# A third raw weight buffer, the first expert's weights split later and in thirds, and a planner's extra delay kept for its lowest rank alone

## Chip, cores, metric

One core of one Trainium2 chip runs the whole program. The metric is device time in microseconds (us): the median of three runs, 2241.27 us before (2236.84 to 2241.68). TensorE is called PE (PEld for its weight loads), VectorE DVE, ScalarE ACT, GpSimd POOL, and SyncE, which issues the DMAs, SP.

## What is computed

A gated linear attention feeds a mixture of experts, which feeds a last block with a cosine:

```python
for t in range(S):                                   # attention, B=4 H=8 S=768 D=48
    state = alpha[:, :, t, :, None] * state + k_t (x) v_t
    y[:, :, t] = q_t @ state
x = y as [3072, 384]
P = exp(x @ w_gate - max)                            # then 8 rounds of row and column scaling
out = sum over 8 experts e of P[:, e:e+1] * (relu(x @ w1[e]) @ w2[e])       # 1024 hidden
h = out @ w_in                                       # 2048 hidden
return (h * cos(h)) @ w_out
```

## The kernel before

**Tiles.** Tokens run along the free dimension. The attention goes by units of 256 tokens (12 units) and, in each, by 4 pairs of heads: 48 slots. `ew` prepares a slot two slots ahead: on DVE two scans along segments of 32 tokens, scalings and a reciprocal, on POOL three 128x256 products or differences, on ACT copies. The slot itself makes on PE 4 transposes (112 columns), 8 score products (48x48), 8 key-value products (64x64) and, one slot later, 8 output products (48x64); DVE puts a mask on the scores (two copy_predicated) and steps the state (four 128x48 scalar_tensor_tensor), ACT copies.

**Passes.** The experts are passes 0 to 7, the two halves of the last block passes 8 and 9. A pass holds its weights in 4 chunks (c) of two matrices (i = 0 first layer, 1 second), each split in a high part (fp32r) and a low part: names w<c><i>h and w<c><i>l, 128x768 each. A product is three: high by high, high by low, low by high. `Passes.first` makes 9 matmuls for one of 8 hidden tiles (ft), then the activation (`act_relu`: ACT writes the high part, DVE the low part; `cos` in passes 8 and 9: four ACT, four DVE and one POOL instruction), and `Passes.second`, two hidden tiles later (three in the last passes), 9 matmuls of the second layer (12 with 384 columns in passes 8 and 9). Pass 0 has 256-token blocks that run between the slots of the attention, as soon as a unit's four slots are done; passes 1 to 9 have 6 blocks of 512 tokens. Pass 0 has 1,728 such matmuls of 256 columns, and 72 more make the gate's logits; `sinkhorn` and `spread` then make the gates P.

**Weights.** `Weights.load` brings a 128x768 piece into one of two raw buffers, `Weights.prep` splits it (ACT copies the high part, POOL subtracts it for the low part) and issues the load for the buffer that it has freed. In the last block of a pass, two preps follow each odd ft. For pass 0 all eight preps stand ahead of the attention's loop.

**Order.** Everything is recorded into `Plan`, which replays it in a simulation of its own with a cost for each instruction (`_cost`) and a latency between engines (`LAT`), and so fixes each engine's order: of the instructions that are ready, the lowest rank first, then the oldest. Attention's slots, activations, evictions and splits of x are rank 0, the passes' matmuls and weight preps rank 1, `ew` and the first preps rank 2, decoding, the adding up of alpha and its loads rank 3. `rank(r, True)` also makes an instruction wait for the last recorded matmul (a floor). What a consumer gets as extra delay in that simulation stands in `Plan.issue`:

```python
same = self.ops[u][0] == e
late = 0 if same or not self.ops[u][6] or self.ops[u][0] == "tensor" else 4000 if e == "sync" else 2500
ready[u] = max(ready[u], t + cost + ((0 if e == "tensor" else 60) if same else self.LAT[e]) + late)
```

`ops[u][6]` is the consumer's rank: every consumer of rank 1 or more, but matmuls, is taken to be ready 2500 ns later (4000 ns behind a DMA) than the latency says. On the chip each engine then works off its list in order. All instructions are issued on line 180, so groups of the profile are told by tiles.

Of the kernel before, what the change touches and what calls it, by code (L numbers as in the profile page):

```python
# [9 lines left out]
F32 = mybir.dt.float32  # L10
# [5 lines left out]
ALU = mybir.AluOpType  # L16
# [3 lines left out]
B, H, S, D = 4, 8, 768, 48  # L20
# [3 lines left out]
E = 8  # L24
NPAIR = H // 2
CH = 64
NPASS = E + 2
NCH = 4
FT = 8
NT = NTOK // 128  # L30
UN = 256
UNITS = [(b, s, UN) for b in range(B) for s in range(0, S, UN)]
BLK = 512
CW = 768
AMIN, AMAX = 0.25, 1.0
LAG = 2
LAG3 = 3
NRAW = 2
FARENA, RARENA = 10000, 10240
SEG = 32  # L40
SCAN = (SEG + 1) * (UN // SEG)
DBG = None
# [20 lines left out]
class Plan:  # L63
# [81 lines left out]
    def issue(self):  # L145
        n = len(self.ops)
        left = [len(o[5]) for o in self.ops]
        users = [[] for _ in range(n)]
        for i, o in enumerate(self.ops):
            for j in o[5]:  # L150
                users[j].append(i)
        ready = [0.0] * n
        cand = {e: [] for e in self.LAT}
        free = dict.fromkeys(self.LAT, 0.0)
        for i, o in enumerate(self.ops):
            if not left[i]:
                cand[o[0]].append(i)
        self.times = [0.0] * n
        for _ in range(n):
            best = None  # L160
            for e, c in cand.items():
                if not c:
                    continue
                t = max(free[e], min(ready[i] for i in c))
                if best is None or t < best[0]:
                    best = t, e
            t, e = best
            i = min((i for i in cand[e] if ready[i] <= t), key=lambda i: (self.ops[i][6], i))
            cand[e].remove(i)
            eng, name, args, kw, cost, _, _ = self.ops[i]  # L170
            self.times[i] = t
            free[e] = t + cost
            for u in users[i]:
                same = self.ops[u][0] == e
                late = 0 if same or not self.ops[u][6] or self.ops[u][0] == "tensor" else 4000 if e == "sync" else 2500
                ready[u] = max(ready[u], t + cost + ((0 if e == "tensor" else 60) if same else self.LAT[e]) + late)
                left[u] -= 1
                if not left[u]:
                    cand[self.ops[u][0]].append(u)
            getattr(getattr(self.nc, eng), name)(*args, **kw)  # L180
# [10 lines left out]
class Arena:  # L191
# [17 lines left out]
    def ring(self, n, shape, dtype):  # L209
        return ring([self.tile(shape, dtype) for i in range(n)])  # L210
# [8 lines left out]
class Weights:  # L219
# [15 lines left out]
    def prep(self):  # L235

        if self.prepped == len(self.order):
            return
        e = self.k.e
        p, c, i = key = self.order[self.prepped]  # L240
        self.prepped += 1
        r = self.raw.pop(key)
        hi, lo = self.t[key] = self.k.w[c][i]
        e.scalar.copy(hi, r)
        e.gpsimd.tensor_tensor(out=lo, in0=r, in1=hi.bitcast(F32), op=ALU.subtract)
        self.load()


# [63 lines left out]
class Kernel:  # L312
    def __init__(self, tc, ctx, qka, vv, nat, vt, wts, w8, wg, cst, out):
        self.tc, self.nc, self.ctx = tc, tc.nc, ctx
        self.qka, self.vv, self.nat, self.vt, self.wts, self.w8 = qka, vv, nat, vt, wts, w8
        self.wg, self.cst, self.out = wg, cst, out

        def pool(name, bufs):
            return ctx.enter_context(tc.tile_pool(name=name, bufs=bufs))

        const = pool("const", 1)
        self.e = self.nc
        self.w = [[[const.tile([128, CW], F32R, name=f"w{c}{i}{z}") for z in "hl"] for i in range(2)] for c in range(NCH)]
        self.raw = [const.tile([128, CW], F32, name=f"raw{i}") for i in range(NRAW)]
        self.ident = const.tile([128, 128], F32, name="ident")
        self.ones = const.tile([128, 128], F32, name="ones")
        self.Lg = const.tile([128, NT, E], F32, name="Lg")
        self.P = const.tile([128, NT, E], F32, name="P")
        self.pt = ctx.enter_context(tc.tile_pool(name="pt", bufs=1, space=bass.MemoryType.DRAM)).tile([NT * E, 128], F32, name="pt")
        self.w32 = ctx.enter_context(tc.tile_pool(name="w32", bufs=1, space=bass.MemoryType.DRAM)).tile([2, NCH, 2, 128, CW], F32, name="w32")  # L330
        self.fbuf = const.tile([128, FARENA], F32, name="fbuf")
        self.rbuf = const.tile([128, RARENA], F32R, name="rbuf")
        self.mask = const.tile([128, UN], U8, name="mask")
        psum = ctx.enter_context(tc.tile_pool(name="psum", bufs=1, space=PSUM))
        self.bank = [psum.tile([128, 512], F32, name=f"bank{i}") for i in range(8)]
        self.flag = const.tile([1, 1], I32, name="flag")
        self.x = const.tile([128, KT, NTOK], F32, name="x")
        self.acc = const.tile([128, KT, NTOK], F32, name="acc")
# [48 lines left out]
    def attention(self, pool):  # L387
        e = self.e
        V, A, G, T, SP = e.vector, e.scalar, e.gpsimd, e.tensor, e.sync
        nt0 = UN // CH  # L390
# [2 lines left out]
        xt = pool.ring(4, [128, 2, UN], F32)  # L393

        decs, fwds, bwd, self.heads = pool.ring(2, [128, SCAN + 1], F32), pool.ring(2, [128, SCAN], F32), pool.tile([128, SCAN + 1], F32), pool.tile([128, SCAN], F32)
        rps, tots = pool.ring(2, [128, UN // SEG], F32), pool.ring(3, [128, nt0], F32)
        kts = pool.ring(2, [128, nt0, D], F32)
        yts = pool.ring(1, [128, UN], F32)
        adev = pool.tile([128, NPAIR * len(UNITS)], F32)
        m1, m2 = tots()[:, 0:1], tots()[0:1, 0:1]  # L400

        late = [Arena(self.acc[:, k, NTOK - 4 * UN:]) for k in range(KT)]

        k6s, mask = late[0].ring(3, [128, UN + CH], F32), self.mask
        qka = ring([z.tile([128, 3, UN], F32) for z in late[1:] + [pool, pool]])
        pt0 = self.bank[0][:, :nt0 * 112].rearrange("p (t d) -> p t d", d=112)
        pk = self.bank[2][:, :nt0 * D].rearrange("p (t d) -> p t d", d=D)
        pg0, py0 = (self.bank[i][:, :UN] for i in (1, 3))
# [73 lines left out]
        for i in range(len(slots) + 1):  # L482
# [3 lines left out]
            if i < len(slots):  # L486
# [6 lines left out]
                t, k6, X, tot = st["qk"], st["k6"], st["X"], st["tot"]  # L493
# [94 lines left out]

    def sinkhorn(self, sm, ps):
        V, A, T = self.e.vector, self.e.scalar, self.e.tensor  # L590
        P, Lg, ones = self.P, self.Lg, self.ones
        self.rank(0)
        mx, nm, m1 = (sm.tile([128, 1], F32) for _ in range(3))
        m1 = m1[0:1]
        rs, rr = sm.tile([128, NT], F32, name="rs"), sm.tile([128, NT], F32, name="rr")
        cs, rc = sm.tile([128, E], F32, name="cs"), sm.tile([128, E], F32, name="rc")
        V.tensor_reduce(out=mx, in_=Lg.rearrange("p t e -> p (t e)"), axis=AX.X, op=ALU.max)
        T.transpose(ps[0:1, 0:128], mx, self.ident)
        V.tensor_reduce(out=m1, in_=ps[0:1, 0:128], axis=AX.X, op=ALU.max)
        T.matmul(ps[:, 0:1], ones[0:1, :], m1, start=True, stop=True)  # L600
        V.tensor_scalar(out=nm, in0=ps[:, 0:1], scalar1=-1.0, scalar2=None, op0=ALU.mult)
        A.activation(P, Lg, AF.Exp, bias=nm)
        for _ in range(8):
            V.tensor_reduce(out=rs, in_=P, axis=AX.X, op=ALU.add)
            V.tensor_scalar(out=rs, in0=rs, scalar1=1e-9, scalar2=None, op0=ALU.add)
            V.reciprocal(rr, rs)
            V.tensor_tensor(out=P, in0=P, in1=rr.unsqueeze(2).to_broadcast([128, NT, E]), op=ALU.mult)
            T.matmul(ps[:, 0:NT * E], ones, P.rearrange("p t e -> p (t e)"), start=True, stop=True)
            V.tensor_reduce(out=cs, in_=ps[:, 0:NT * E].rearrange("p (t e) -> p e t", e=E), axis=AX.X, op=ALU.add)
            V.tensor_scalar(out=cs, in0=cs, scalar1=1e-9, scalar2=None, op0=ALU.add)  # L610
            V.reciprocal(rc, cs)
            V.scalar_tensor_tensor(out=P, in0=P, scalar=float(NTOK // E), in1=rc.unsqueeze(1).to_broadcast([128, NT, E]), op0=ALU.mult, op1=ALU.mult)
# [17 lines left out]

    def stage1(self):
        e, pool, rp = self.e, Arena(self.fbuf), Arena(self.rbuf)
        e.vector.memset(self.ones, 1.0)
        at = self.attention(pool)

        def pump(_=0):
            next(at, None)
# [16 lines left out]
        self.rank(2)  # L654
        for _ in range(NRAW):
            w.load()
        for _ in range(2 * NCH):
            w.prep()
        self.gate_weights(wgs)
        for ui, (b, s0, n) in enumerate(UNITS):  # L660
            while self.done <= ui:
# [10 lines left out]
            if not left:  # L672
                sm = Arena(self.fbuf)
# [220 lines left out]
```

## Time and profile before

| | us |
|---|---|
| median of three runs | 2241.27 |
| profiled execution, its own time | 2242.62 |
| its span, first to last instruction | 2240.7 |
| PE busy | 2176.2 (97%) |
| DVE busy | 1092.9 (49%) |
| POOL busy | 818.3 (37%) |
| ACT busy | 797.3 (36%) |

The sum of the prediction is made against the profiled execution. What lies around its span is 1.9 us, and its time is 1.35 us above the median. A busy PE is not a PE at its peak, since the ends of matmuls are modelled. Some matmul records are missing, so counts of matmuls in a stretch are compared with counts, not with the program.

### The profile page before, as it was taken

How to read it: one execution, taken by the hardware profiler on the slowest of the kernel's cores; microseconds unless marked ns; L12 is line 12 of the kernel's file. 1: busy time of each engine (PE TensorE's matmuls, PEld its weight loads, DVE VectorE, ACT ScalarE, POOL GpSimd, SP SyncE). 2: the span in 40 equal slices, each digit the busy share in tenths (PEclk: the TensorE clock that was granted, in tenths of full speed). 3: DMA queues.
4: the chain of work that ended last, by engine and by line, in shares of the span. 5: the costliest groups of instructions: out<-in, count | busy, mean ns of one | idle time of the engine just before them, and what ended most of it. 6: DMA issues, size and time to landing. Idle time of an engine off the chain costs nothing.

```text
span 2240.7 us, 31634 instructions
## 1 busy us (share of the span) xinstructions
PE 2176.2 (97%) x12406; PEld 1848.9 (83%) x12406; DVE 1092.9 (49%) x2113; ACT 797.3 (36%) x1724; POOL 818.3 (37%) x688
## 2 busy tenths in 40 slices
PE   6899999999999999999999999999999989998998
PEld 5788889888888888888888888888888879987997
DVE  8898885122133343334325334333431257774775
ACT  4666663322222222222212212222221255664664
POOL 5544441443332243233224322422432353454442
PEclk9999999999999999999999999999999989998999
DMA  4322210210121021012102101100110010000000
GB/s 133 96 83 76 77 61 3 75 27 15 35 64 26 21 80 33 25 48 61 31 21 66 48 21 52 61 25 28 61 45 5 22 32 4 1 22 22 29 29 30
DMA packets 70703, 94.85 MB, mean 42 GB/s; under 512 B 6992, under 2 KB 52624, under 8 KB 70544
## 3 DMA queue, kind: packets, MB, share of 16 engines
q1 hardware_dynamic: 70544, 92.74, 14.0%
q8 instruction: 99, 1.62, 0.3%
q14 instruction: 60, 0.49, 0.1%
HBM read 80.42 MB, written 11.11 MB: 41 GB/s over the span
## 4 chain that ended last, share of the span: by engine, by line
PE 88%; DVE 9%; ACT 2%; issue 1%; DMA 0%; SPq 0%; POOL 0%; DVEq 0%; ACTq 0%; POOLq 0%
PE bank L180 88%; DVE fbuf L180 7%; ACT fbuf L180 1%; DVE acc L180 1%; DVE rbuf L180 1%; ACT rbuf L180 0%; DMA fbuf<-in_cst_dram 0%; DVE x L180 0%; ACT x L180 0%; ACT acc L180 0%; SPq L180 0%; DVE Lg L180 0%; POOL rbuf L180 0%; DVEq L180 0%; ACTq L180 0%
## 5 line engine op out<-in xcount | busy, mean ns | idle before, releaser
L180 DVE SCALAR_TENSOR_TENSOR rbuf<-bank,rbuf 128x512 fp32r<-128x512 f32 (+1 forms) x432 | 271.3, 629 | 788.0 <-ACT rbuf L180 787.0
L180 ACT ACTIVATE rbuf<-bank 128x512 fp32r<-128x512 f32 (+1 forms) x432 | 237.4, 550 | 1030.7 <-PE bank L180 1024.2
L180 POOL TENSOR_TENSOR rbuf<-x,rbuf 128x512 fp32r<-128x512 f32 (+1 forms) x162 | 189.4, 1191 | 677.6 <-ACT rbuf L180 642.2
L180 POOL TENSOR_TENSOR acc<-acc,fbuf 128x512 f32<-128x512 f32 (+1 forms) x216 | 241.6, 1142 | 283.2 <-DVE fbuf L180 228.8
L180 PE MATMUL bank<-rbuf,w01h 128*128 128x512 f32 (+1 forms) x648 | 202.3, 369 | 0.0
L180 PE MATMUL bank<-rbuf,w11h 128*128 128x512 f32 (+1 forms) x648 | 202.1, 369 | 0.1
L180 PE MATMUL bank<-rbuf,w10h 128*128 128x512 f32 (+1 forms) x792 | 194.7, 377 | 7.4 <-DVE fbuf L180 7.1
L180 PE MATMUL bank<-rbuf,w21h 128*128 128x512 f32 (+1 forms) x648 | 201.6, 368 | 0.0
L180 DVE TENSOR_SCALAR fbuf<-fbuf 128x192 uint32<-128x192 uint32 (+4 forms) x264 | 150.3, 589 | 104.1 <-ACT fbuf L180 103.3
L180 PE MATMUL bank<-rbuf,w31h 128*128 128x512 f32 (+1 forms) x648 | 200.2, 369 | 0.0
L180 POOL TENSOR_TENSOR rbuf<-fbuf,rbuf 128x512 fp32r<-128x512 f32 x96 | 128.4, 1342 | 196.0 <-ACT rbuf L180 193.6
L180 PE MATMUL bank<-rbuf,w20h 128*128 128x512 f32 (+1 forms) x792 | 193.2, 376 | 4.1 <-DVE rbuf L180 4.0
L180 PE MATMUL bank<-rbuf,w00h 128*128 128x512 f32 (+1 forms) x792 | 195.4, 380 | 1.8 <-DVE rbuf L180 1.8
L180 PE MATMUL bank<-rbuf,w30h 128*128 128x512 f32 (+1 forms) x792 | 190.6, 374 | 1.9 <-DVE rbuf L180 1.7
L180 DVE SCALAR_TENSOR_TENSOR fbuf<-fbuf 128x192 uint32<-128x192 uint32 (+2 forms) x288 | 188.3, 654 | 6.1
L180 PEld LDWEIGHTS bank<-rbuf,w10h 128*128 128x128 f32 x792 | 141.7, 190 | 33.8 <-DVE fbuf L180 8.1
L180 PEld LDWEIGHTS bank<-rbuf,w00h 128*128 128x128 f32 x792 | 144.3, 193 | 28.5 <-DVE rbuf L180 2.8
L180 PEld LDWEIGHTS bank<-rbuf,w20h 128*128 128x128 f32 x792 | 141.8, 190 | 30.6 <-DVE rbuf L180 4.8
L180 PEld LDWEIGHTS bank<-rbuf,w30h 128*128 128x128 f32 x792 | 141.5, 189 | 28.4 <-DVE rbuf L180 2.9
L180 ACT ACTIVATE fbuf<-fbuf 128x512 f32<-128x512 f32 (+1 forms) x216 | 139.9, 648 | 54.9 <-DVE fbuf L180 52.7
L180 DVE TENSOR_TENSOR fbuf<-bank,fbuf 128x512 f32<-128x512 f32 x126 | 82.9, 685 | 150.1 <-PE bank L180 150.0
L180 PEld LDWEIGHTS bank<-rbuf,w11h 128*128 128x128 f32 x648 | 119.1, 189 | 21.0 <-ACT rbuf L180 0.7
(119 smaller groups left out, 3864.3 us busy)
## 6 DMA issues: line engine op xcount, KB each, us to landing
raw<-in_wts_dram SPq DMA_DIRECT2D x64, 384.0 KB, 3.3
fbuf<-pt SPq DMA_DIRECT2D x48, 256.0 KB, 4.8
fbuf<-in_w_dram SPq DMA_DIRECT2D x64, 192.0 KB, 2.9
acc<-in_qka_dram SPq DMA_DIRECT2D x24, 384.0 KB, 3.1
fbuf<-in_qka_dram SPq DMA_DIRECT2D x24, 384.0 KB, 3.4
w<-fbuf SPq DMA_DIRECT2D x64, 96.0 KB, 1.6
raw<-w SPq DMA_DIRECT2D x16, 384.0 KB, 3.0
fbuf<-in_vv_dram SPq DMA_DIRECT2D x24, 192.0 KB, 3.2
```

Source lines behind the costliest of these rows:

```text
L180: getattr(getattr(self.nc, eng), name)(*args, **kw)
```

## The change

Three raw buffers in place of two, for which P, ones and some of the attention's small tiles move into memory that is free at that time (the last quarter of acc, and the scratch of `sinkhorn`), and the float arena shrinks from 10000 to 9480 columns. The low part of every weight is made in three POOL instructions of 256 columns. The eight preps of pass 0 stand between the first 12 steps of the attention's generator (three slots), two for each three steps, with rank 3 and a floor. The extra delay goes to consumers of rank 3 alone.

```diff
-NRAW = 2
-FARENA, RARENA = 10000, 10240
+NRAW = 3
+FARENA, RARENA = 9480, 10240
...
-                late = 0 if same or not self.ops[u][6] or self.ops[u][0] == "tensor" else 4000 if e == "sync" else 2500
+                late = 0 if same or self.ops[u][6] < 3 else 4000 if e == "sync" else 2500
...
-        e.gpsimd.tensor_tensor(out=lo, in0=r, in1=hi.bitcast(F32), op=ALU.subtract)
+        for o in range(0, CW, 256):
+            t = slice(o, o + 256)
+            e.gpsimd.tensor_tensor(out=lo[:, t], in0=r[:, t], in1=hi[:, t].bitcast(F32), op=ALU.subtract)
...
+        adev, rps = late[0].tile([128, NPAIR * len(UNITS)], F32), late[0].ring(2, [128, UN // SEG], F32)
+        yts, tots = late[1].ring(1, [128, UN], F32), late[2].ring(3, [128, nt0], F32)
+        kts = ring([z.tile([128, nt0, D], F32) for z in (late[2], pool)])
...
+        P, ones = sm.tile([128, NT, E], F32), sm.tile([128, 128], F32)
+        self.P = P
         self.rank(0)
+        V.memset(ones, 1.0)
...
-        for _ in range(2 * NCH):
+        for i in range(2 * NCH):
+            if i % 2 == 0:
+                for _ in range(3):
+                    pump()
+            self.rank(3, True)
             w.prep()
+        self.rank(2)
```

The line on `late` changes the planner's order on every engine. Two places show it. The first is PE's order in the attention, around the start of pass 0's second block; bank_92 (bank_91 in the change) takes a slot's transposes, 48x48 are its scores, 64x64 its key-value products, 48x64 its outputs, and 128x256 are matmuls of pass 0. Before:

```order
L180 MATMUL bank_98<-rbuf,w31h 128x256
L180 MATMUL bank_98<-rbuf,w31l 128x256
L180 MATMUL bank_98<-rbuf,w31h 128x256 x2
L180 MATMUL bank_98<-rbuf,w31l 128x256
L180 MATMUL bank_98<-rbuf,w31h 128x256
L180 MATMUL bank_99<-rbuf,w31h 128x256
L180 MATMUL bank_99<-rbuf,w31l 128x256
L180 MATMUL bank_92<-ident,acc 128x112 x3
L180 MATMUL bank_99<-rbuf,w31h 128x256
L180 MATMUL bank_96<-rbuf,w10h 128x256 x6
L180 MATMUL bank_96<-rbuf,w10l 128x256 x3
```

The change:

```order
L180 MATMUL bank_98<-rbuf,w31h 128x256
L180 MATMUL bank_91<-ident,acc 128x112 x3
L180 MATMUL bank_94<-fbuf 48x64 x8
L180 MATMUL bank_91<-ident,acc 128x112
L180 MATMUL bank_93<-fbuf 48x48 x8
L180 MATMUL bank_95<-rbuf,w00h 128x256 x6
L180 MATMUL bank_95<-rbuf,w00l 128x256 x3
L180 MATMUL bank_92<-acc 64x64 x8
L180 MATMUL bank_97<-rbuf,w31l 128x256
L180 MATMUL bank_97<-rbuf,w31h 128x256 x2
```

Between a slot's products stand fewer matmuls of pass 0. Counted over PE's whole order, 1,272 of the 1,800 matmuls of 256 columns (pass 0 and the gate) stand before the attention's last output product before, and 604 in the change; on DVE 67 of the 96 low parts of act_relu stand before the attention's last state step before, and 32 in the change.

The second place is PE's order in pass 8's last block; 128x512 are matmuls of the first layer, 128x384 of the second. Before, the six high ones of two hidden tiles stand together:

```order
L180 MATMUL bank_93<-rbuf,w20h 128x512 x6
L180 MATMUL bank_99<-rbuf,w20h 128x512 x6
L180 MATMUL bank_94<-w11h,rbuf 128x384
L180 MATMUL bank_95<-w11h,rbuf 128x384
L180 MATMUL bank_96<-w11h,rbuf 128x384
L180 MATMUL bank_97<-w11h,rbuf 128x384
L180 MATMUL bank_97<-w11l,rbuf 128x384
```

and their three low ones some 20 rows further on, after nearly all of the second layer's matmuls for two older tiles:

```order
L180 MATMUL bank_97<-w11h,rbuf 128x384
L180 MATMUL bank_97<-w11l,rbuf 128x384
L180 MATMUL bank_93<-rbuf,w20l 128x512 x3
L180 MATMUL bank_99<-rbuf,w20l 128x512 x3
L180 MATMUL bank_97<-w11h,rbuf 128x384
```

The change, at the same place:

```order
L180 MATMUL bank_96<-w01h,rbuf 128x384
L180 MATMUL bank_96<-w01l,rbuf 128x384
L180 MATMUL bank_96<-w01h,rbuf 128x384
L180 MATMUL bank_98<-rbuf,w20h 128x512 x6
L180 MATMUL bank_98<-rbuf,w20l 128x512 x3
L180 MATMUL bank_93<-w11h,rbuf 128x384
L180 MATMUL bank_93<-w11l,rbuf 128x384
```

Each tile's nine first-layer matmuls stand together, one tile of the first layer alternates with one of the second, and so it is in all blocks of passes 1 to 9. Before, low matmuls put off in this way also stood in the last block of each of the passes 1 to 7.

## Rows read from the trace of the kernel before

**Rows 1.** Busy time by stretch: length, then PE, PEld, DVE, ACT, POOL (instructions), clock, DMA

```profile
0.00:348.00 348.00, 310.18 (x3793) 274.99 (x3794) 298.12 (x799) 212.38 (x719) 161.97 (x213) 0.99 0.28 85
348.00:416.00 68.00, 68.00 (x560) 66.95 (x559) 31.86 (x101) 21.48 (x58) 16.98 (x14) 1.00 0.10 25
416.00:1800.00 1384.00, 1383.56 (x6041) 1133.94 (x6040) 472.76 (x781) 309.60 (x523) 440.98 (x321) 1.00 0.14 39
1800.00:2096.00 296.00, 277.38 (x1326) 248.53 (x1325) 195.59 (x286) 172.71 (x290) 144.31 (x102) 0.95 0.06 18
2096.00:2240.70 144.70, 137.08 (x695) 124.54 (x693) 94.61 (x149) 81.13 (x136) 54.03 (x41) 0.99 0.08 29
```

**Rows 2.** The page's chain that ended last, by engine

```profile
PE 88%; DVE 9%; ACT 2%; issue 1%; DMA 0%; SPq 0%; POOL 0%; DVEq 0%; ACTq 0%; POOLq 0%
```

**Rows 3.** DVE and POOL groups from 0 to 348: busy us, mean ns, idle before

```profile
L180 DVE TENSOR_TENSOR_SCAN fbuf<-fbuf 128x264 f32<-128x264 f32 x96 | 76.8, 824 | 1.3
L180 DVE SCALAR_TENSOR_TENSOR rbuf<-bank,rbuf 128x256 fp32r<-128x256 f32 x68 | 27.8, 414 | 10.0 <-ACT rbuf L180 9.6
L180 POOL TENSOR_TENSOR rbuf<-x,rbuf 128x256 fp32r<-128x256 f32 x35 | 28.6, 818 | 94.1 <-ACT rbuf L180 84.4 <-DVE fbuf L180 7.4 <-DMA fbuf<-in_qka_dram 2.3
L180 POOL TENSOR_TENSOR w01l<-raw,w01h 128x768 fp32r<-128x768 f32 x1 | 2.2, 2207 | 0.0
```

**Rows 4.** What DVE waited for, 0 to 348: total us, times, longest

```profile
DVE fbuf L180 <- PE bank L180: 22.0, 20, 3.2
DVE rbuf L180 <- ACT rbuf L180: 9.6, 11, 2.1
DVE fbuf L180 <- ACT fbuf L180: 5.3, 11, 0.7
```

**Rows 5.** ACT's group of pass 0's activations, 396.4 to 411.3

```profile
L180 ACT ACTIVATE rbuf<-bank 128x256 fp32r<-128x256 f32 x7 | 2.7, 384 | 6.9 <-PE bank L180 6.7
```

**Rows 6.** Busy time by stretch in passes 8 and 9, columns as in the first group

```profile
1820.00:1845.00 25.00, 17.39 (x66) 14.74 (x65) 12.65 (x17) 12.31 (x21) 11.27 (x8) 0.80 0.10 32
1845.00:1878.00 33.00, 33.00 (x160) 29.85 (x159) 23.12 (x33) 19.45 (x33) 15.21 (x12) 0.95 0.04 13
1878.00:1911.00 33.00, 33.00 (x168) 29.92 (x167) 22.89 (x37) 20.57 (x35) 14.43 (x12) 1.00 0.00 1
...
2030.00:2045.00 15.00, 9.74 (x42) 8.42 (x41) 4.71 (x8) 5.61 (x10) 5.70 (x5) 0.84 0.18 52
2045.00:2062.00 17.00, 13.58 (x54) 11.70 (x53) 6.80 (x11) 7.96 (x15) 8.58 (x7) 0.80 0.00 1
2062.00:2095.00 33.00, 33.00 (x155) 29.46 (x154) 20.25 (x33) 18.79 (x32) 14.89 (x11) 0.93 0.07 25
```

**Rows 7.** What PE waited for, 1800 to 2096

```profile
PE bank L180 <- ACT rbuf L180: 11.5, 3, 5.3
PE bank L180 <- DVE fbuf L180: 7.1, 3, 3.4
```

**Rows 8.** Timeline of DVE and POOL in pass 8's last block: start, us, instruction

```profile
1996.11 0.68 DVE L180 SCALAR_TENSOR_TENSOR fbuf<-fbuf 128x512 f32<-128x512 f32 x1
...
1999.38 2.26 DVE L180 SCALAR_TENSOR_TENSOR fbuf<-fbuf 128x512 f32<-128x512 f32 x1
...
1999.24 1.85 POOL L180 TENSOR_TENSOR w01l<-raw,w01h 128x768 fp32r<-128x768 f32 x1 [0.97 <-ACT w01h L180]
```

**Rows 9.** The page's DMA issues: weights into a raw buffer, us to landing

```profile
raw<-in_wts_dram SPq DMA_DIRECT2D x64, 384.0 KB, 3.3
```

**Rows 10.** A stretch with a lower clock, and PE's loads of one form there and later

```profile
80.40:83.70 3.30, 3.30 (x40) 2.98 (x39) 3.26 (x4) 1.90 (x7) 3.30 (x4) 0.50 0.02 5
...
L180 PEld LDWEIGHTS bank<-fbuf 64*48 64x48 f32 x16 | 1.2, 191 | 0.2 <-ACT fbuf L180 0.2
...
L180 PEld LDWEIGHTS bank<-fbuf 64*48 64x48 f32 x542 | 18.3, 121 | 5.8 <-DVE fbuf L180 1.5 <-issue 1.1 <-ACT fbuf L180 0.4
```

More of the change, by code (lines that the diff above doesn't have):

```diff
@@ L325, in __init__ @@
         self.ident = const.tile([128, 128], F32, name="ident")
-        self.ones = const.tile([128, 128], F32, name="ones")
         self.Lg = const.tile([128, NT, E], F32, name="Lg")
-        self.P = const.tile([128, NT, E], F32, name="P")
         self.pt = ctx.enter_context(tc.tile_pool(name="pt", bufs=1, space=bass.MemoryType.DRAM)).tile([NT * E, 128], F32, name="pt")
@@ L395, in attention @@
         decs, fwds, bwd, self.heads = pool.ring(2, [128, SCAN + 1], F32), pool.ring(2, [128, SCAN], F32), pool.tile([128, SCAN + 1], F32), pool.tile([128, SCAN], F32)
[L396 to L400, printed above, removed]
         late = [Arena(self.acc[:, k, NTOK - 4 * UN:]) for k in range(KT)]
@@ L405, in attention @@
         qka = ring([z.tile([128, 3, UN], F32) for z in late[1:] + [pool, pool]])
+        adev, rps = late[0].tile([128, NPAIR * len(UNITS)], F32), late[0].ring(2, [128, UN // SEG], F32)
+        yts, tots = late[1].ring(1, [128, UN], F32), late[2].ring(3, [128, nt0], F32)
+        kts = ring([z.tile([128, nt0, D], F32) for z in (late[2], pool)])
+        m1, m2 = tots()[:, 0:1], tots()[0:1, 0:1]
         pt0 = self.bank[0][:, :nt0 * 112].rearrange("p (t d) -> p t d", d=112)
@@ L590, in sinkhorn @@
         V, A, T = self.e.vector, self.e.scalar, self.e.tensor
-        P, Lg, ones = self.P, self.Lg, self.ones
+        Lg = self.Lg
+        P, ones = sm.tile([128, NT, E], F32), sm.tile([128, 128], F32)
+        self.P = P
         self.rank(0)
+        V.memset(ones, 1.0)
         mx, nm, m1 = (sm.tile([128, 1], F32) for _ in range(3))
@@ L632, in stage1 @@
         e, pool, rp = self.e, Arena(self.fbuf), Arena(self.rbuf)
-        e.vector.memset(self.ones, 1.0)
         at = self.attention(pool)
```

## The prediction

> **What bounds the kernel now.** First the chain of waits: 88% of it is PE and 9% DVE [rows 2]. So the end is set by PE's work plus the stretches in which PE is not fed. Second, the busy time by stretch, to see where those lie [rows 1]. From 416 to 1800 us (passes 1 to 7) PE is busy 1383.56 of 1384.00 us: nothing can be won there. From 0 to 348 (attention with pass 0 between its slots) DVE is busy 298.1 us and PE counts 310.2, but far fewer matmuls per us than later. From 348 to 416 PE alone works off the rest of pass 0 and the gates. From 1800 on PE is again short of work: 277.4 busy of 296, at a granted clock of 0.95. The change can act in two places only: the first 416 us, and passes 8 and 9.
>
> Third, what holds the attention. DVE's waits show only 22.0 us for PE, 9.6 for the high parts of act_relu and 5.3 for ACT's copies [rows 4]; 298.1 of 348 us it works, on its two scans per slot (96 x 824 ns = 77 us) and much else [rows 3]. So the attention goes at DVE's pace, and pass 0's matmuls fill PE between the slots. What doesn't fit is paid at the end, on PE alone.
>
> **Part 1, the planner's delay, first 416 us.** The order on PE (above) says what moves: 1,272 of 1,800 matmuls of 256 columns stand before the attention's last output product, and 604 in the change. 668 are put behind the attention. Behind it they have no cover: seven activations, so seven pairs of 9 and 9 matmuls, take 14.9 us there [rows 5], which is 2.13 us per 18, or 118 ns each. 668 x 0.118 = **79 us more** after the attention.
>
> Against this the attention ends sooner. DVE's order has 32 low parts of act_relu before the last state step in place of 67: 35 x 0.414 us [rows 3] = 14.5, so DVE's work is 298.1 - 14.5 = 283.6 us. Its idle time was 348 - 298.1 = 49.9. Of that I scale the wait for PE with the matmuls in between (22.0 x 604/1272 = 10.4), that for act_relu with its count (9.6 x 32/67 = 4.6), and keep the 5.3 and the other 13.0, which hold the start. That makes 33.3, and the attention ends at 283.6 + 33.3 = 317, **31 us sooner**. PE does not hinder it: 348 us less 1,272 x 0.118 = 150 leave at most 198 us for the attention's own matmuls, and 198 + 604 x 0.118 = 269 is below 317. So some 48 us of PE's time in the attention stay empty, where matmuls stood before. Why the planner does this can be read from its costs: it counts a scan as 67 + 2.1 x 264 = 621 ns where DVE takes 824 [rows 3], and the delay of 2500 ns, now gone for `ew` (rank 2), made up for it. It now takes the attention to be quicker than DVE is, and lets it run ahead of pass 0.
>
> Stage 1 together: +79 - 31 = **+48 us**. Bounds: if only the 13.0 us of idle remain, the attention ends at 297 and the sum is +28; if all 49.9 remain, at 333.5, and it is +64. I take the middle, since the relation of DVE's waits to the matmuls in front of it is the one thing the rows show.
>
> **Part 2, the same delay, passes 8 and 9.** In a clean stretch 168 matmul records take 33 us, 5.09 per us [rows 6]. From 1820 to 1878 there are 226 in 58 us, worth 44.4: 13.6 us are lost. From 2030 to 2095 there are 251 in 65 us, worth 49.3: 15.7 lost. Together **29 us**, of which 18.6 are waits for high parts of the cosine and for DVE [rows 7] and the rest the granted clock of 0.80 to 0.95 in and behind them [rows 6]. The order explains them: the planner took the low parts of the weights to be late (delay of 2500 ns for rank 1, 4000 behind a load), put off the low matmuls of two tiles, and so started both cosines late, with nothing left to do meanwhile. The change puts each tile's nine matmuls together and alternates the layers. The weights do come in time for that: a load lands in 3.3 us [rows 9], a split takes some 3 us (POOL up to 2.2, and ACT before it), and two tiles, which need one pair of weights, about 8 (a block of 8 tiles is 33 us) [rows 3, 6]. I take 25 of 29 back, since preps still share ACT and POOL with the cosine there. Bounds: 29, and 8 if only half of the second stretch is cured.
>
> **Part 3, three POOL instructions for one.** 256 columns take about 818 ns, so three take 2.45 us, against 1.85 to 2.2 for 768 columns [rows 3, 8]: at most 0.6 us each, 80 times 48 us of POOL, which is idle most of the time in passes 1 to 7 and has 8 of them (5 us) in the attention. Zero on the path there. In passes 8 and 9 they help: DVE's step of 0.68 us took 2.26 beside a split of 1.85 [rows 8]. That is within the 25. The Trainium skill (SBUF — State Buffer, Who interferes with whom) states that DVE and GpSimd share a port pair by an exclusive lock for a whole instruction. The trace agrees (2.26 beside 1.85); by that rule the longest hold falls to a third, all 29 us would come back, and the sum would be 4 us lower.
>
> **The rest.** The third raw buffer starts a load earlier that landed in 3.3 us anyway: zero but for Part 2. The moved small tiles and the later memset of ones are a few instructions before waits that DVE has anyway: zero, bounded by 1 us either way. The later first splits free ACT and POOL in the first 40 us; pass 0's first matmuls come two slots later, which is already in the count of 604.
>
> **Sum.** 2242.6 (the profiled execution) + 48 - 25 = 2265.6; it lies 1.35 us above the median of the runs, so **2264 us**, 1.0% slower. About 0.2%, 4.5 us, is what a measurement of this kernel can tell from no change.
>
> **Rivals.**
> *The attention tightens more (faster).* If POOL's instructions stretch DVE less, DVE's 283.6 us themselves shrink. At 0.6 us less per slot the attention ends at 317 - 29 = 288: +79 - 60 - 28 = -9, or 2232 us. It decides as soon as the attention ends before 294 (79 less 25 is 54). For it: DVE's step of 2.26 beside 0.68 [rows 8]. Against it: the slots' POOL work is unchanged and is pressed into less time. Chance 0.16.
> *The order does not act as counted (no change).* If the two parts are each small or cancel, with the attention ending near 294, the time is 2241. For it: PE was counted busy 310 of 348 [rows 1], so its gaps may be worth less than I think. Chance 0.10.
> *The stalls of the last passes stay.* The cosine has ten instructions in a row, and the first loss (from 1820) lies where passes change from relu to cosine whatever the order. Then 8 of 29 come back: +40, or 2281. Chance 0.14.
> *PE's clock falls in the attention.* With fewer matmuls in between, PE is emptier. From 80.4 to 83.7 the granted clock was 0.50 (1.2 GHz), and a weight load took 191 in place of 121 ns [rows 10]. At 1.6 times, PE's 269 us would be 430 if the whole attention ran so, above DVE's 317; a quarter of it at that level adds some 28: 2292. The Trainium skill (TensorE: Matmul & The Clock Gate, Part 1) states that the throttled clock is the default and that activity releases it, which speaks against this change; the trace agrees, in that the low clock stands only in stretches with gaps. Chance 0.10.
> My forecast has 0.50.
>
> **Range and chances.** From 2234 (the first rival's neighbourhood, and the lower bounds of both parts: +28 - 29 = -1 is 2240) to 2292 (the clock, and +64 - 8 = +56 is just outside). Slower by over 0.2%: forecast, stalls and clock, 0.50 + 0.14 + 0.10 = 0.74. Within 0.2%: 0.10. Faster: 0.16.
>
> **What would show it.** Right: the attention's last DVE step near 317 us, PE alone for some 147 us behind it (68 + 79), the first 512-column activation near 464 in place of 416; DVE's wait for PE about half of 22.0; passes 8 and 9 with stalls of a few us in place of 18.6 and a clock near 1.0. Wrong: an attention that ends before 294, or a stretch behind it that is much shorter than 147 us; stalls after 1800 as before.

## The result, and the profile after

| | before | change |
|---|---|---|
| median, us | 2240.57 (2236.84 to 2241.68, 4 runs) | 2263.84 (2262.84 to 2265.87, 4 runs) |
| profiled execution, its span | 2240.7 | 2261.0 |
| PE busy | 2176.2 (97%) | 2199.5 (97%) |

The ratio is 1.0111 (95% interval 1.0097 to 1.0125): 1.1% slower. The number is the one predicted; the way to it is not, as the stretches show. Busy time by stretch in the change (columns as in [rows 1]; the cuts are the attention's last copy into x on ACT, the first block of pass 1, and the start of pass 8):

```profile
0.00:293.40 293.40, 239.95 (x3115) 206.84 (x3116) 269.42 (x759) 193.22 (x647) 159.79 (x218) 0.89 0.33 102
293.40:442.00 148.60, 148.30 (x1236) 146.32 (x1236) 47.28 (x140) 48.40 (x133) 31.63 (x36) 1.00 0.07 19
442.00:1850.00 1408.00, 1408.00 (x6036) 1131.03 (x6035) 457.19 (x779) 312.64 (x524) 454.16 (x434) 1.00 0.13 38
1850.00:2261.00 411.00, 403.24 (x2024) 363.73 (x2022) 289.79 (x435) 251.06 (x423) 201.15 (x162) 1.00 0.06 20
```

Against [rows 1]: the attention ends at 293 instead of 348 us, the stretch of PE alone behind it is 149 instead of 68 long, and both were foreseen in kind. The third line was not. PE is busy without a gap in both kernels, and does the same work, but 6036 matmuls take 1408 us (233.3 ns each), where [rows 1] had 6041 in 1384 (229.1). No record is missing in this count: both traces hold all 6,912 matmuls of 512 columns that passes 1 to 9 have. The last line has only 8 us without PE, in place of some 26 in the last two lines of [rows 1].

Stage 1 ends, for this text, at the first activation of 512 columns on ACT. Its rows in the timeline, of the change:

```profile
442.70 0.60 ACT L180 ACTIVATE rbuf<-bank 128x512 fp32r<-128x512 f32 x1 [0.36 <-PE bank L180]
```

and of the kernel before:

```profile
416.64 0.60 ACT L180 ACTIVATE rbuf<-bank 128x512 fp32r<-128x512 f32 x1 [1.04 <-PE bank L180]
```

Cut there and at the first cosine of pass 8, the difference of the two spans (20.3 us) is:

| us | before | change | difference | predicted |
|---|---|---|---|---|
| stage 1 (attention, pass 0, gates) | 416.6 | 442.7 | +26.1 | +48 |
| passes 1 to 7 | 1381.9 | 1407.0 | +25.1 | 0 |
| passes 8 and 9 | 442.2 | 411.3 | -30.9 | -25 |

DVE's waits in the attention, up to 293.4 (total us, times, longest), against [rows 4]:

```profile
DVE fbuf L180 <- PE bank L180: 7.3, 7, 2.6
DVE rbuf L180 <- ACT rbuf L180: 2.9, 2, 1.5
DVE fbuf L180 <- ACT fbuf L180: 1.6, 3, 0.7
```

They are 11.8 us in place of 36.9, and DVE works 269.4 of 293.4 us. From 1800 on PE's list of waits has one line left of [rows 7]:

```profile
PE bank L180 <- ACT rbuf L180: 0.4, 1, 0.4
```

Pass 8's start and pass 9's start in the change, where [rows 6] had PE busy 17.4 of 25 and 9.7 of 15 us:

```profile
1850.00:1883.00 33.00, 33.00 (x161) 28.95 (x160) 26.48 (x36) 20.54 (x36) 25.19 (x22) 1.00 0.12 37
...
2050.00:2083.00 33.00, 33.00 (x168) 29.82 (x167) 24.19 (x35) 22.14 (x37) 26.82 (x26) 1.00 0.09 24
```

No gap is left, at a granted clock of 1.00.

### The profile page after: what moved, and what is told of

Its sections match the earlier page's. It is cut to its first block, busy times and chain, and to the rows that moved or that the text cites. A ratio compares the mean times of both kernels' runs of the same rounds, so it can differ in the third digit from the quotient of the medians.

```text
span 2261.0 us, 31949 instructions
## 1 busy us (share of the span) xinstructions
PE 2199.5 (97%) x12406; PEld 1847.9 (82%) x12406; DVE 1063.7 (47%) x2113; ACT 805.3 (36%) x1724; POOL 846.7 (37%) x848
## 4 chain that ended last, share of the span: by engine, by line
PE 89%; DVE 10%; issue 1%; ACT 0%; POOL 0%; DVEq 0%; POOLq 0%; ACTq 0%
PE bank L180 89%; DVE fbuf L180 8%; DVE acc L180 1%; DVE rbuf L180 0%; ACT fbuf L180 0%; POOL acc L180 0%; DVE x L180 0%; POOL w30l L180 0%; ACT acc L180 0%; ACT rbuf L180 0%; DVE bank L180 0%; ACT x L180 0%; DVE Lg L180 0%; DVE mask L180 0%; DVEq L180 0%
## 5 line engine op out<-in xcount | busy, mean ns | idle before, releaser
L180 POOL TENSOR_TENSOR acc<-acc,fbuf 128x512 f32<-128x512 f32 (+1 forms) x192 | 224.5, 1192 | 236.6 <-DVE fbuf L180 206.7
L180 DVE TENSOR_SCALAR fbuf<-fbuf 128x192 uint32<-128x192 uint32 (+4 forms) x264 | 162.2, 634 | 87.9 <-ACT fbuf L180 87.2
L180 DVE SCALAR_TENSOR_TENSOR fbuf<-fbuf 128x192 uint32<-128x192 uint32 (+3 forms) x296 | 164.0, 554 | 6.2
L180 PEld LDWEIGHTS bank<-rbuf,w21h 128*128 128x128 f32 x648 | 120.1, 190 | 23.2
```

## Where the slower matmuls come from

In passes 1 to 7 nothing but PE is on the path, so 4.4 ns more per matmul is 6,048 x 4.4 = 27 us (7 passes, 6 blocks, 8 hidden tiles, 18 matmuls). The order there is regular in both kernels, the operands have the same shapes, and the clock is 1.00. What else differs is the work beside PE (splits in thirds on POOL, loads into a third buffer), and an address. The tiles stand one behind the other in SBUF, so the change moves every tile behind the raw buffers: + 3072 bytes per partition for a third raw buffer, - 512 for ones, - 768 for P, - 2080 for an arena shorter by 520 columns: 288 bytes down for rbuf, from 114368 to 114080. rbuf holds the moving operand of all these matmuls, the one that streams through PE; the weights lie ahead of the raw buffers and stay where they are. The first experiments move rbuf (and behind it mask, which the attention alone reads).

**change_rbuf_moved: the change, rbuf 32 bytes up** (114112). The tile flag (32 bytes as laid out) is allocated ahead of rbuf instead of behind it; x and acc stay.

```diff
         self.fbuf = const.tile([128, FARENA], F32, name="fbuf")
+        self.flag = const.tile([1, 1], I32, name="flag")
         self.rbuf = const.tile([128, RARENA], F32R, name="rbuf")
...
-        self.flag = const.tile([1, 1], I32, name="flag")
```

> The changed kernel with the small tile flag allocated ahead of rbuf: rbuf (the tile that holds the split x and the hidden activations, which PE reads) starts 32 bytes later in each partition, at 114112 in place of 114080; x, acc and the order of every instruction stay. Theory (address): the matmuls of passes 1 to 7 take 233.3 ns in the change against 228.9 before because rbuf starts at a multiple of 32 bytes that is none of 64; then they are back at 228.9, passes 1 to 7 are 25 us shorter and the time is 2239 +- 4. Rival (work beside): thirds on POOL or the third buffer's loads disturb PE; then nothing moves, 2264 +- 2.

Measured: 2233.99 us, ratio to before 0.9968 (0.9958 to 0.9978). Its stretches:

```profile
0.00:293.10 293.10, 237.32 (x3115) 203.87 (x3116) 270.23 (x759) 192.86 (x647) 160.01 (x218) 0.92 0.33 102
293.10:442.20 149.10, 148.81 (x1237) 146.84 (x1236) 47.32 (x140) 48.38 (x134) 31.68 (x36) 1.00 0.08 19
442.20:1823.00 1380.80, 1380.80 (x6034) 1132.91 (x6034) 458.52 (x779) 312.59 (x523) 453.79 (x433) 1.00 0.14 39
```

Stage 1 is that of the change to 0.3 us; passes 1 to 7 are 27 us shorter, with the same work beside them: that rival is out.

**before_rbuf_moved: the kernel before, rbuf 32 bytes up** (114400), by the same edit.

> The kernel before with the same move: rbuf starts at 114400 in place of 114368, x and acc stay, no instruction changes place. Theory (address): matmuls of passes 1 to 7 go from 228.9 to about 233.3 ns, +25 us, 2266 +- 4. Rival (work beside): nothing moves, 2240.6 +- 2.

Measured: 2267.02 us, 1.0115 (1.0098 to 1.0132). Passes 1 to 7 take 1408.6 us. In the same 600 us of them, all of it busy, the kernel before and this run count:

```profile
600.00:1200.00 600.00, 600.00 (x2623) 492.32 (x2622) 223.02 (x375) 132.58 (x225) 184.28 (x133) 1.00 0.15 43
...
600.00:1200.00 600.00, 600.00 (x2573) 482.67 (x2572) 213.59 (x364) 130.22 (x221) 179.18 (x131) 1.00 0.14 40
```

So the address alone makes the one kernel 30 us faster and the other 25 us slower. That it does is shown both ways; by what rule was the next question. The two good addresses were multiples of 64, the two bad ones 32 past one.

**change_rbuf_at_512: the change with rbuf at 114176.** This and the next two change one number, which moves rbuf, acc and x together (PE reads neither acc nor x in passes 1 to 7):

```diff
-FARENA, RARENA = 9480, 10240
+FARENA, RARENA = 9504, 10240
```

> The change with an arena larger by 24 columns (9504 in place of 9480), which moves rbuf, acc and x up by 96 bytes: rbuf stands at 114176, a multiple of 512. Nothing else moves. If the 32 bytes past a multiple of 64 are all that costs time, it is as change_rbuf_moved: 228.9 ns between matmuls of 512 columns, and 2234 us. Rival: the distance to a larger boundary counts too; before's address (114368) and that of change_rbuf_moved (114112) are multiples of 64, and the latter of 256, so a multiple of 512 would go below 228.9 ns by 1 ns or more, and the time to 2228 or less.

Measured: 2266.29 us (1.0114, 1.0097 to 1.0131). A multiple of 512 is as bad as 32 past a multiple of 64: **my rule fell.** (114112 is no multiple of 256, as the expectation has it; it is 192 past one, like 114368.) What was left was the place within 128 bytes, 64 for both good addresses.

**change_rbuf_at_64_of_256** (FARENA 9520, rbuf at 114240):

> The change with an arena of 9520 columns: rbuf at 114240, 64 past a multiple of 256. The multiple of 64 alone has fallen (114176 is one, and the change ran at 233.3 ns there); the addresses with 228.9 ns, 114112 and 114368, are both 64 past a multiple of 128 and 192 past one of 256. If the place within 128 bytes decides, this is at 228.9 ns and 2234 us. Rivals: the place within 256 decides, or any other property of the two good addresses, or the move of x and acc that comes with a larger arena: 233.3 ns and 2264 to 2268 us.

**change_rbuf_at_128_of_256** (FARENA 9536, rbuf at 114304):

> The change with an arena of 9536 columns: rbuf at 114304, a multiple of 128 but not of 256. If the place within 128 bytes decides, this is as 114176: a rhythm of two (229 and 238 ns), 233.3 ns on the mean, 2266 us. Rival, the place within 256 or a larger block decides: another rhythm, and if it is 228.9 ns, 2234 us.

Measured: 2259.26 us (1.0079, 1.0062 to 1.0095) and 2226.07 us (0.9934, 0.9917 to 0.9951). Both expectations missed: the place that was to be good is slow (233.3 ns, as its rivals had it, though the time is 5 us below theirs), and the one that was to be slow is faster than any other address. The count of matmuls in the same 600 us shows it, with PE busy throughout. The change:

```profile
600.00:1200.00 600.00, 600.00 (x2573) 482.00 (x2572) 205.82 (x358) 132.21 (x221) 188.41 (x180) 1.00 0.14 41
```

and change_rbuf_at_128_of_256, the same program 224 bytes further up:

```profile
600.00:1200.00 600.00, 600.00 (x2649) 496.82 (x2648) 213.72 (x371) 136.74 (x229) 195.95 (x188) 1.00 0.15 41
```

The times from one matmul's start to the next, in ns, read from single matmuls at 900 us, are a pattern that repeats without end:

```
rbuf at   kernel                      repeated pattern      mean    passes 1-7
114080    change                      235 233 234 231       233.3   1407.0 us
114112    change_rbuf_moved           226 229 232           228.9   1380.2
114176    change_rbuf_at_512          229 238               233.3   1407.0
114240    change_rbuf_at_64_of_256    233 233 234           233.3   1407.0
114304    change_rbuf_at_128_of_256   226 227 227           226.7   1366.8
114368    before                      226 229 232           228.9   1381.9
114400    before_rbuf_moved           231 232 237           233.3   1408.6
```

The pattern runs on over the tiles of nine matmuls and over both layers, and over 1400 us: PE goes at a fixed rhythm. In these seven runs the rhythm went with rbuf's address; seven addresses gave six patterns and three means, and none of the rules that I tried (multiples of 64, place within 128) holds. The rule stays open, and so does what in the chip makes the rhythm.

The ranking is that of 512 columns alone. Pass 0's matmuls of 256 columns, back to back behind the attention, took 115.4 ns on the mean at 114240, 117.7 at 114112 and 119.8 at 114304 (gaps left out): the address that is best for 512 is the slowest of the change's five there. Stage 1 ends at 439.4, 442.9 and 444.5 us in these three runs.

## Which part of the change does the rest

**before_delay_rank_3: the kernel before with the planner's line alone** (two raw buffers, whole splits, first preps ahead, rbuf at 114368; matmuls stay exempt, whatever their rank, which the change's own line drops).

```diff
-                late = 0 if same or not self.ops[u][6] or self.ops[u][0] == "tensor" else 4000 if e == "sync" else 2500
+                late = 0 if same or self.ops[u][6] < 3 or self.ops[u][0] == "tensor" else 4000 if e == "sync" else 2500
```

> The kernel before with the new rule for the delay alone (rank 3 only): two raw buffers, 768-column splits on POOL, first preps as before, rbuf where it was. 604 matmuls of pass 0 stand before the attention's last output product. Theory (the rule alone makes both parts): attention ends near 295 us, stage 1 is 26 us longer, passes 8 and 9 lose under 5 us in place of 30, passes 1 to 7 stay at 228.9 ns: 2240.6 + 26 - 28 = 2239 +- 6. Rival (the third buffer or the thirds are what cures passes 8 and 9): stalls of 10 us or more remain there, 2250 or more.

Measured: 2238.61 us, 0.9994 (0.9984 to 1.0004): no difference, made of two that cancel. Its stretches:

```profile
0.00:298.80 298.80, 240.97 (x3129) 206.92 (x3130) 277.45 (x760) 193.98 (x651) 154.04 (x202) 0.92 0.32 99
298.80:446.50 147.70, 147.40 (x1223) 145.40 (x1223) 46.92 (x139) 45.70 (x128) 29.97 (x28) 1.00 0.08 19
446.50:1828.00 1381.50, 1381.50 (x6037) 1133.50 (x6037) 468.84 (x780) 312.95 (x525) 439.10 (x320) 1.00 0.14 39
1828.00:2236.00 408.00, 401.04 (x2022) 363.67 (x2020) 286.25 (x435) 250.67 (x422) 194.43 (x140) 1.00 0.06 20
```

Stage 1 ends at 447.2 (+30.6), and passes 8 and 9 take 409.4 us (-32.8). The line makes both the loss and the cure; neither the third buffer nor the thirds are needed for the cure.

**change_delay_ranks_2_3: the change, with the delay kept for `ew` too** (rbuf at 114080).

```diff
-                late = 0 if same or self.ops[u][6] < 3 else 4000 if e == "sync" else 2500
+                late = 0 if same or self.ops[u][6] < 2 else 4000 if e == "sync" else 2500
```

> The changed kernel with the extra delay given to consumers of rank 2 too (2 and 3; none for rank 1). 1312 matmuls of pass 0 then stand before the attention's last output product (1344 with the gate's), against 596 in the change. Theory (the delay for ew decides the balance): the attention ends near 348 us again, the first 512-column activation is near 416 in place of 443, passes 8 and 9 stay without stalls, and the time is 26 us under the change: 2238 +- 6. Rival (the later and lower-ranked first preps cost the start): the attention does not win back its 26 us, 2255 or more.

Measured: 2226.65 us, 0.9936 (0.9919 to 0.9952). Its first two stretches:

```profile
0.00:347.50 347.50, 314.46 (x3876) 283.60 (x3877) 294.87 (x803) 217.51 (x727) 169.07 (x229) 0.99 0.28 86
347.50:409.00 61.50, 60.90 (x488) 59.18 (x487) 29.93 (x96) 20.77 (x56) 18.05 (x20) 1.00 0.14 34
```

PE has 3876 matmuls beside the attention again, against 3115 in the change, and stage 1 ends at 409.7: 33.0 us are rank 2's delay alone. Passes 8 and 9 stay cured (411.7), so their stalls came from rank 1's delay. It came out 11 us better than I expected, as stage 1 is 7 us shorter than before's, and passes 1 to 7 some 3 us shorter than the change's (1404.2).

**before_delay_ranks_2_3: the kernel before with its line alone changed.**

```diff
-                late = 0 if same or not self.ops[u][6] or self.ops[u][0] == "tensor" else 4000 if e == "sync" else 2500
+                late = 0 if same or self.ops[u][6] < 2 or self.ops[u][0] == "tensor" else 4000 if e == "sync" else 2500
```

> The kernel before with one line changed: the planner's delay goes to ranks 2 and 3 instead of 1 to 3. Two raw buffers, whole splits of 768 columns, first preps ahead of the attention, rbuf at before's address. If rank 2's delay sets the balance of the attention and rank 1's the stalls of passes 8 and 9, the attention with its tail ends as before (416 us, give or take 5) and passes 8 and 9 lose their 31 to 33 us: 2206 to 2214. Rival: the third raw buffer and the thirds are what lets passes 8 and 9 run without stalls once the attention is balanced so: the stalls stay and the time is 2230 or more.

Measured: 2202.52 us, 0.9831 (0.9814 to 0.9847): one line in the kernel before is worth 38 us. Stage 1 ends at 414.1, passes 8 and 9 take 409.2. The time is 3 us under what I expected, as passes 1 to 7 are shorter too (1378.0). The stalls don't come back with two raw buffers and whole splits: that rival is out.

**change_both_edits: the change with the edits of change_rbuf_moved and change_delay_ranks_2_3** (rbuf at 114112).

```diff
-                late = 0 if same or self.ops[u][6] < 3 else 4000 if e == "sync" else 2500
+                late = 0 if same or self.ops[u][6] < 2 else 4000 if e == "sync" else 2500
...
+        self.flag = const.tile([1, 1], I32, name="flag")
         self.rbuf = const.tile([128, RARENA], F32R, name="rbuf")
...
-        self.flag = const.tile([1, 1], I32, name="flag")
```

> The change with both edits of before: rbuf moved up by 32 bytes to a multiple of 64 (one tile allocated ahead of it), and the planner's extra delay for ranks 2 and 3 instead of rank 3 alone. The order on every engine is that of change_delay_ranks_2_3 (2226.65 us). If rbuf's address costs each matmul of 512 columns about 4.4 ns wherever the order stands, this run's spacing is 228.9 ns, passes 1 to 7 take 1380 us in place of 1404, and the time is 2226.65 - 26 to 30 = 2197 to 2201 us. Rival: the two gains overlap (the slow matmuls stood under work that the new order does not have), and the time is 2210 or more.

Measured: 2198.18 us, 0.9813 (0.9796 to 0.9829). Of five executions four took 2197.1 to 2199.4, but the profiled one 2226.58, with 233.3 ns per matmul at an address that had given 228.9 in every other run. Up to 411 us its pattern is 226 229 232; then come two short waits (0.39 and 0.43 us). PE's weight loads there, from the timeline (start, us, instruction, idle before and what ended it):

```profile
411.01 0.19 PEld L180 LDWEIGHTS bank<-rbuf,w01h 128*128 128x128 f32 x1 [0.39 <-ACT rbuf L180]
411.12 0.19 PEld L180 LDWEIGHTS bank<-rbuf,w01l 128*128 128x128 f32 x1
411.73 0.30 PEld L180 LDWEIGHTS bank<-rbuf,w01h 128*128 128x128 f32 x2 [0.43 <-DVE rbuf L180]
```

Behind them it is 233 233 234 for 1400 us, until passes 8 and 9 with their 384-column matmuls break it up.

**change_both_edits_again: the same kernel once more.**

> The same kernel as change_both_edits, whose profiled execution fell into 233.33 ns per matmul after a short wait of PE at 411 us (2226.6 us), and whose four other executions took 2197 to 2199. If the rhythm is chosen by what happens at that wait and not by the address alone, most executions are at 2198, with 228.9 ns between 450 and 1750 us, and one in some may be at 2226. Rival: the profiled execution was disturbed by something else, and none is at 2226.

Measured: 2198.38 us, all four executions between 2198.0 and 2198.9. At the same place the profile shows the same waits (0.36 and 0.43 us), and the pattern behind them is 226 229 232 with a nanosecond of jitter. So one address can hold two rhythms, and the one profile that shows both has the change at these two waits. None of these four executions is at 2226, as the rival had it; with one such execution in nine, that doesn't decide between the two. That the waits were the cause is the nearest reading, and not shown: I made no run that puts a wait there on purpose.

**change_both_edits_whole_splits: as change_both_edits, with one POOL instruction of 768 columns per split.**

```diff
-        for o in range(0, CW, 256):
-            t = slice(o, o + 256)
-            e.gpsimd.tensor_tensor(out=lo[:, t], in0=r[:, t], in1=hi[:, t].bitcast(F32), op=ALU.subtract)
+        e.gpsimd.tensor_tensor(out=lo, in0=r, in1=hi.bitcast(F32), op=ALU.subtract)
```

> As change_both_edits, but the low part of a weight is made in one POOL instruction of 768 columns instead of three of 256. The prediction costed the thirds at nothing on the path of passes 1 to 7 and at a help in passes 8 and 9 (within the 25 us taken back). If so, this is 0 to 4 us slower than change_both_edits (2197 to 2205). Rival: three instructions cost more than one on POOL and hold ACT or DVE in the attention, and one alone is faster by 3 us or more.

Measured: 2202.77 us, 0.9835 (0.9819 to 0.9852), 4.6 us slower than change_both_edits by the medians. Not where I had put it: stage 1 ends at 409.4 (408.8 in change_both_edits_again), passes 8 and 9 take 410.0 in both, and the rest (1380.3 against 1377.3) lies between. It is also little more than a measurement of this kernel can tell (4.5 us), and the two intervals overlap. The planner orders some of PE's matmuls otherwise with these splits, so I can't say how much of it is the splits themselves.

**both_edits_early_splits: as change_both_edits, with the first eight splits ahead of the attention, as before.**

```diff
-        for i in range(2 * NCH):
-            if i % 2 == 0:
-                for _ in range(3):
-                    pump()
-            self.rank(3, True)
+        for _ in range(2 * NCH):
             w.prep()
-        self.rank(2)
```

> change_both_edits with the eight first splits ahead of the attention's loop again, as in the kernel before. Against before_delay_ranks_2_3 it differs by the third raw buffer and the thirds, against change_both_edits by the place of the first splits alone. If the later first splits are what made stage 1 some 4 us shorter (410.4 us to the first activation of 512 columns, against 414.1), this has 414 us there and 2202 us. Rival: it is the buffer, the thirds or chance of the order, and this is within 1.5 us of change_both_edits.

Measured: **2195.78 us**, 0.9796 (0.9780 to 0.9813), the lowest median of all: 46 us below before and 68 below the change. Both readings of the expectation missed: it is faster than change_both_edits, by some 2.5 us. Its first two stretches:

```profile
0.00:348.40 348.40, 317.20 (x3895) 284.86 (x3896) 284.99 (x804) 218.39 (x731) 166.50 (x229) 0.98 0.28 86
348.40:404.00 55.60, 55.60 (x456) 54.63 (x456) 29.55 (x95) 19.58 (x51) 16.63 (x18) 1.00 0.10 31
```

Stage 1 ends at 404.8, earlier than with the later splits (408.8): the later first splits cost about 4 us of stage 1 rather than save them, of which 2.6 us show in the whole (2195.78 against 2198.38; all four executions of the one lie below all four of the other). Against before_delay_ranks_2_3 (414.1) the third buffer, the moved tiles and the thirds together are worth some 9 us of stage 1 and 6.7 us of the whole.

## Why the prediction was right, and where it was not

The forecast of 2264 was met by 2263.84, and that was luck. Its sum was +23 from two terms, and these two came to -5 (26.1 - 30.9). The other 25 us were in no term and no rival. change_rbuf_moved is the change as I had understood it: 2234 us, 0.3% faster than before and at the lower end of the range. The sign that I forecast was that of an address. By the prediction's own signs it was wrong: an attention that ends before 294 was to show that, and it ended at 293.4; the first 512-column activation came at 442.7, not near 464.

**The step that failed** is "The rest": "The third raw buffer [...]: zero but for Part 2" and "The moved small tiles [...]: zero, bounded by 1 us", with "nothing can be won there" for passes 1 to 7. I costed the buffer by its loads and the moved tiles by their instructions, and took PE's busy 1383.56 of 1384.00 for a floor. It said only that PE had no gap. Whoever moves a tile moves all that stand behind it, and passes 1 to 7 went from 1381.9 to 1407.0, and with rbuf 32 bytes up they take 1380.2. No row of before could have priced that, but the shift of 288 bytes could be read from the diff.

**Part 1** was right in its mechanism, and mis-sized. The tail is 442.7 - 293.4 = 149 us, predicted 147. The attention ended at 293.4, not 317. 14 of the 24 us are DVE's work (269.4, predicted 283.6): besides the low parts of act_relu (33 are left, 13.3 us), most other steps became shorter, and some longer, the 64x128 ones from fbuf most. Four groups of DVE, 0 to 348, in the kernel before:

```profile
L180 DVE TENSOR_TENSOR fbuf<-fbuf 64x128 f32<-64x128 f32 x48 | 17.6, 366 | 0.5
L180 DVE TENSOR_TENSOR fbuf<-fbuf 128x4 f32<-128x4 f32 x48 | 17.4, 363 | 0.0
L180 DVE TENSOR_TENSOR fbuf<-fbuf 128x256 f32<-128x256 f32 x24 | 15.3, 637 | 0.2
L180 DVE TENSOR_TENSOR acc<-acc,fbuf 128x256 f32<-128x256 f32 x24 | 13.6, 568 | 0.0
```

and in the change, 0 to 293.4:

```profile
L180 DVE TENSOR_TENSOR fbuf<-fbuf 64x128 f32<-64x128 f32 x48 | 21.3, 444 | 0.6
L180 DVE TENSOR_TENSOR acc<-fbuf 128x4 f32<-128x4 f32 x48 | 13.4, 279 | 0.6
L180 DVE SCALAR_TENSOR_TENSOR rbuf<-bank,rbuf 128x256 fp32r<-128x256 f32 x33 | 13.3, 408 | 3.1 <-ACT rbuf L180 2.9
L180 DVE TENSOR_TENSOR fbuf<-fbuf 128x256 f32<-128x256 f32 x24 | 12.5, 522 | 0.1
L180 DVE TENSOR_TENSOR acc<-acc,fbuf 128x256 f32<-128x256 f32 x24 | 11.8, 490 | 0.0
```

The first rival had this mechanism (DVE's steps stretch less), at half its size, and its point of decision was reached. Single instructions of the two traces bear it out. A TENSOR_TENSOR of 128x256 with no POOL instruction at work beside it took the same in both (422 and 420 ns), one with a POOL instruction beside it took more (656 and 579), and 37 of 48 stand beside one before, 26 in the change. For 128x4 it is 149 and 155 ns without, 491 and 550 with, and 30 and 15 of 48. The 64x128 steps meet POOL more often (44 and 71 of 96), and one of their two groups became longer. POOL's whole work in the attention is nearly the same (162.0 and 159.8 us) and pressed into less time, so what changed is which steps it meets. Some 6 of the 14 us come with the planner's line (DVE's work is 277.45 in before_delay_rank_3), the other 8 with the rest of the change; by which edit, the runs don't show. The other 9 us are idle time: 24.0, predicted 33.3, as the waits fell faster than the count of matmuls between (for PE 7.3, predicted 10.4; for ACT's copies 1.6, where I had kept 5.3).

**Part 2** was right in its mechanism: predicted 25 us with an upper bound of 29, measured 30.9. Its reason, the order made by rank 1's delay, is shown by before_delay_rank_3, which has that alone. The help that I gave the thirds there isn't borne out: with whole splits passes 8 and 9 take 409.4, 409.2 and 410.0, with thirds 409.5 to 413.8. Beside Part 3 stood a rule of the Trainium skill (SBUF — State Buffer, Who interferes with whom): DVE and GpSimd share a port pair by an exclusive lock for a whole instruction. By it shorter POOL instructions were to bring back the last 4 us. All of the loss did come back, but with whole splits as well, so passes 8 and 9 don't tell for or against that rule; they show that the stalls go without shorter holds.

**The clock rival** came half true. Three stretches of the change's attention:

```profile
110.00:120.00 10.00, 8.39 (x78) 7.15 (x77) 9.81 (x29) 6.32 (x22) 6.15 (x9) 0.72 0.46 150
...
160.00:170.00 10.00, 9.66 (x83) 8.61 (x84) 9.71 (x26) 6.31 (x22) 6.02 (x8) 0.55 0.37 105
...
220.00:230.00 10.00, 9.91 (x111) 8.42 (x109) 7.29 (x21) 5.57 (x21) 4.11 (x8) 0.65 0.29 92
```

The granted clock is 0.55 to 0.72 there, and 0.89 over the whole attention, against 0.99 before. Between two levels, 0.5 and 1.0 (the trace has no other), a mean of 0.89 is 22% of the time at the lower one: nearly the quarter that the rival priced at 28 us. In the first two stretches DVE is at work 9.8 and 9.7 of 10 us all the same; in the third it waits 2.6 us for PE. All of DVE's waits for PE and ACT in the attention are 11.8 us, so the clock cost at most that. In change_rbuf_moved, with the same order and 0.92, the attention ends at 293.1, 0.3 us sooner. The rival's price, PE slower than DVE, was what didn't happen.

**The stalls of the last passes stay**: out, PE's waits after 1800 are 0.4 us. **The order cancels** came nearer than any other rival, and I had given it 0.10. It names two parts that cancel with an attention that ends near 294; it ended at 293.4, and the parts come to -5 us in the change and to -2 in before_delay_rank_3. But they are large, 26 us or more each, and its ground (PE's gaps are worth less than I think) is not what made them cancel.

**Three readings of the prediction were wrong**, though no term of the sum rests on them. [rows 1] has more matmuls per us in the attention (3793 in 348 us) than later (6041 in 1384), small ones; only those of pass 0 are fewer. The cosine has nine instructions, not ten. And the low clock doesn't stand in stretches with gaps only: in [rows 10] it is 0.50 with PE busy for 3.30 of 3.30 us, and in [rows 6] it is still 0.95 behind a gap, with PE busy for 33.00 of 33.

## What to carry to other kernels

An engine that is busy all the time can still become slower: compare counts in a stretch of equal length (2573 against 2623 matmuls in 600 us), not busy shares alone. When a change adds, drops or resizes a tile, write down what moves behind it, and test the change once with the address of the hot operand put back; otherwise a gain or a loss of 1% is put down to the wrong edit. And a planner's delay that is made to balance one stage should be set for that stage's rank: here rank 2's was worth 33 us and rank 1's cost 31 to 33, and one line had moved both.

## What the runs showed of the hardware that was not expected

Matmuls of 128x512 back to back, at a granted clock of 1.00 and with no wait, took 226.7, 228.9 or 233.3 ns on the mean, in fixed patterns of two to four matmuls that lasted 1400 us. The pattern went with the address of the moving operand in steps of 32 bytes, by no rule that seven addresses would show, and the best address for 512 columns was the slowest of the change's five for 256. Of the 26 timed executions of the four kernels that have it at 114112 one was some 28 us longer, and its profile shows 233.3 for 228.9.

In the attention of the kernel before, many of DVE's steps that read SBUF alone took longer beside a POOL instruction (422 and 656 ns for the TENSOR_TENSOR of 128x256, 288 and 503 for the TENSOR_SCALAR, 700 and 873 for the scan); those that read a bank did not (414 and 413 ns for the low parts of act_relu, 443 and 443 for the mask).

The best address (114304) and the best order (both_edits_early_splits) were not tried together. An estimate from their passes 1 to 7 (1366.8 against 1380.2 us), with 2 us back for passes 8 and 9 (411.9 against 409.5) and 2 for stage 1 (444.5 against 442.9 in change_rbuf_moved), is 2186 us.
